# ScalarE seeds an accumulating PSUM bank with the first of seven products, and VectorE's first add falls away

## The chip, the cores and the metric

The kernel runs on one core of one Trainium2 chip. The metric is the device time of one execution in microseconds (us), lower is better. The kernel is written by hand in a low-level language: every instruction is issued to one engine (TensorE, ScalarE, VectorE, GpSimd, or SyncE for transfers), each engine executes its own instructions in order, and engines wait for each other through semaphores.

## The reference

Linformer attention followed by a gated feed-forward layer, in float32:

```
k_proj = einsum('ks,bhsd->bhkd', E, k)         # 8 batches, 8 heads, 1024 tokens, 64 per head
v_proj = einsum('ks,bhsd->bhkd', F, v)
attn   = softmax(q @ k_proj^T / 8)
x      = (attn @ v_proj), heads joined         # 8192 tokens x 512
gate   = 1 / (1 + exp(-(x @ w_gate)))          # 512 x 1536
val    = x @ w_val                             # 512 x 1536
out    = (gate * val) @ w_out                  # 1536 x 512
```

## The kernel before, in words

The kernel multiplies in bf16 and accumulates in fp32 in PSUM. PSUM has eight banks, each holding a 128 x 512 fp32 tile. Four of them, pF0 to pF3, serve the feed-forward layer; pA0 to pA3 serve attention and the output product.

The 8192 tokens are cut into 16 blocks of 512. Block 0 goes through the feed-forward layer plainly (`mstep`: 12 steps, each with a G product and a V product of four matmuls, then `gate`). For blocks 1 to 15 the value product x @ w_val is done by a Strassen-like scheme: a block and the weights are cut into 2 x 2 parts, and seven products of sums replace eight. The sums of x lie in `xS`, those of the weights in `vT` and in part of `wV`. One *group* K (3 to 47, 45 groups, three to a block) makes four of the twelve 128-row strips of the hidden layer, and `v_pieces(K)` writes its seven products as five pieces. Two banks, called a and c in the code, are held through the group:

- p1: product A11·B11 into bank a (four matmuls of 256 columns). `v_snap(0, a)`: ScalarE copies a into the SBUF tile `vsnap0`. Bank a keeps its contents, and later products accumulate onto it.
- p26: product A12·B21 into bank c; `v_add(0, c)`: VectorE adds bank c to `vsnap0`. Then S2·T2 onto bank a and `v_snap(1, a)`. Then `hidden(K, 0, 0)`: VectorE multiplies the finished quarter by its gate and writes a quarter of `hT`.
- p57: S1·T1 into bank c, from the start; S3·T3 onto a; `v_snap(2, a)`; `v_add(2, c)`.
- p4: A22·T4 onto a; `hidden(K, 0, 1)` straight from bank a; `hidden(K, 1, 1)` from `vsnap2`.
- p3: S4·B22 onto c; `v_add(1, c)`; `hidden(K, 1, 0)` from `vsnap1`.

Between these pieces stand the gate products `g_step(K, n)`, n = 0 to 3: four matmuls of 512 columns into a bank of their own, and a tanh on ScalarE into a `sig` tile. The order on TensorE around a group is p3 of the group before, p1, g1, p26, g2, p57, g3, p4, g0 of the next group, p3. That order is written out by hand in `quad_pieces`, and `on(u, j, ...)` hangs other work behind chosen pieces: attention's scores, their exponentials and products (`scores3`, `mixed3`, `outputs3`), VectorE's sums for later blocks (`x_sums`, `h_sums`), and the output product, which is also done with seven products (`first_products`, `last_products`, 24 matmuls each before the next piece).

The banks pF0 to pF3 are handed out by a first-in-first-out list `FF`: `take()` takes the head, `two()` takes two, and a step appends its bank when it has emitted the instruction that reads it last. The list fixes, while the program is built, which earlier reader a bank's next writer waits for. `Plan.add` derives those waits from the keys of each operation. In its argument list, `x` marks a bank that an operation uses alone, `r` a key that it reads and `w` a key that it writes. All matmuls are recorded under line 264 and all ScalarE operations under line 268 (helpers `mm` and `act`), `v_add` under L1476, `hidden` under L1457, `gate` of block 0 under L1133.

Of the kernel before, what the change touches and what calls it, by code (L numbers as in the profile page):

```python
# [6 lines left out]
AF = mybir.ActivationFunctionType  # L7
# [20 lines left out]
class Plan:  # L28
# [9 lines left out]
    def add(self, eng, fn, r=(), w=(), x=(), dma=None):  # L38
        op = Op()
        op.eng, op.fn, op.dma, op.need = eng, fn, dma, False  # L40
        op.sem, op.val = None, 0
        deps = {}

        def dep(o, raw):
            if o is op:
                return
            if o.eng == eng and o.dma is None:
                if eng == "PE" or (eng != "POOL" and not raw):
                    return
            deps[id(o)] = o  # L50

        for k in r:
            for o in self.writers.get(k, ()):
                dep(o, True)
        for k in tuple(w) + tuple(x):
            for o in self.writers.get(k, ()):
                dep(o, False)
            for o in self.readers.get(k, ()):
                dep(o, False)
        for k in r:  # L60
            self.readers.setdefault(k, []).append(op)
        for k in tuple(w) + tuple(x):
            self.writers[k] = [op]
            self.readers[k] = []
        op.deps = list(deps.values())
        for o in op.deps:
            o.need = True
        if dma is not None:
            self.dma_count[dma] = self.dma_count.get(dma, 0) + 16
            op.sem, op.val = dma, self.dma_count[dma]  # L70
        self.ops.append(op)
        return op
# [46 lines left out]
def bass_linformer_attn__then__ffn_glu_sigmoid_kernel(  # L119
# [18 lines left out]
    with contextlib.ExitStack() as es:  # L138

        def sbuf(name, shape, dtype):  # L140
            return es.enter_context(nc.sbuf_tensor(name, shape, dtype))
# [7 lines left out]
        def within(shape, dtype):  # L149
# [64 lines left out]
        vsnap = [sbuf(f"vsnap{i}", [P, 512], FP32) for i in range(3)]  # L214
        xS = [sbuf(f"xS{i}", [P, 4, 2, 256], BF16) for i in range(2)]

        bank = [
            es.enter_context(nc.psum_tensor(n, [P, 512], FP32))
            for n in ("pF0", "pF1", "pF2", "pF3", "pA0", "pA1", "pA2", "pA3")
        ]  # L220
# [3 lines left out]
        add = plan.add  # L224
# [29 lines left out]
        FF, AA = Free(), Free()  # L254

        def mm(b, o, lhsT, rhs, r, start=True, stop=True, tp=None, tr=False, read=False):
            kw = {"skip_group_check": True} if read else {}
            if tp is not None:
                kw["tile_position"] = tp
            if tr:  # L260
                kw["is_transpose"] = True
            else:
                kw["start"], kw["stop"] = start, stop
            return add("PE", lambda e: e.matmul(o, lhsT, rhs, **kw), r=r, x=[("bank", b)])  # L264

        def act(o, i, r, w, b=None, func=AF.Copy, scale=1.0):
            x = [] if b is None else [("bank", b)]
            return add("ACT", lambda e: e.activation(o, i, func, scale=scale), r=r, w=w, x=x)  # L268

        def dve(fn, r, w, b=None):  # L270
            x = [] if b is None else [("bank", b)]
            return add("DVE", fn, r=r, w=w, x=x)
# [807 lines left out]
        def chunk(m):  # L1080
            return max(x for x in range(len(WCH) - 1) if WCH[x] <= m * P)
# [319 lines left out]
        def x_part(blk, n):  # L1401
            s, hf = blk // 2 % 2, blk % 2
            if n[0] == "S":
                return xS[blk % 2][:, int(n[1]) - 1, :, :], [("xS", blk % 2, int(n[1]))]
            tok, i0 = int(n[1]) - 1, 2 * (n[2] == "2")
            return (
                xT[s][:, i0 : i0 + 2, hf, 256 * tok : 256 * tok + 256],
                [("xT", s, i0 + i, hf, tok) for i in range(2)],
            )
# [11 lines left out]
        def v_product(blk, q, bk, A, B, start=False, stop=False):  # L1421
            x, kx = x_part(blk, A)
            for j in range(2):
                for i in range(2):
                    m = 2 * q + j
                    if B in ("T2", "T3", "T4"):
                        w, kw = vT[:, int(B[1]) - 2, i, m * P : (m + 1) * P], ("vT", int(B[1]), int(m > 1))
                    else:
                        if B == "T1":
                            ii, mm_, kw = i, m + H6, ("vT", 1, int(m > 1))  # L1430
                        else:
                            ii, mm_ = i + 2 * (B[1] == "2"), m + H6 * (B[2] == "2")
                            kw = ("wV", chunk(mm_), ii // 2)
                        w = wV[:, ii, mm_ * P : (mm_ + 1) * P]
                    mm(
                        bk,
                        bank[bk][:, 256 * j : 256 * j + 256],
                        w,
                        x[:, i, :],
                        kx + [kw],  # L1440
                        start=start and i == 0 and j == 0,
                        stop=stop and i == 1 and j == 1,
                        read=True,
                    )

        def pair(k, half_):
            return sigs[(2 * k + half_) % 3], ("sig", (2 * k + half_) % 3)

        def hidden(K, half_, tok, x, r, b=None):

            blk, q = K // 3, K % 3
            m = 2 * q + H6 * half_
            sg, k = pair(K, half_)
            cc = slice(256 * tok, 256 * tok + 256)
            o = hT[blk % 2][:, m : m + 2, cc]
            dve(
                lambda e: e.scalar_tensor_tensor(  # L1457
                    o,
                    sg[:, :, cc],
                    1.0,  # L1460
                    x.rearrange("p (j c) -> p j c", j=2),
                    ALU.add,
                    ALU.mult,
                ),
                [k + (j,) for j in range(2)] + r,
                [("hT", blk % 2, m + j, tok) for j in range(2)],
                b=b,
            )

        def v_snap(n, bk):  # L1470
            act(vsnap[n][:, :], bank[bk][:, :], [], [("vsnap", n)], b=bk)

        def v_add(n, bk):
            o = vsnap[n][:, :]
            dve(
                lambda e: e.tensor_tensor(o, bank[bk][:, :], o, ALU.add),  # L1476
                [("vsnap", n)],
                [("vsnap", n)],
                b=bk,
            )  # L1480

        held_v = {}
# [19 lines left out]
        def v_pieces(K):  # L1502
            blk, q = K // 3, K % 3

            def p1():
                held_v["a"] = a = FF.take()
                v_product(blk, q, a, "A11", "B11", start=True)
                v_snap(0, a)

            def p26():  # L1510
                a = held_v["a"]
                held_v["c"] = c = FF.take()
                v_product(blk, q, c, "A12", "B21", start=True, stop=True)
                v_add(0, c)
                v_product(blk, q, a, "S2", "T2")
                v_snap(1, a)
                hidden(K, 0, 0, vsnap[0][:, :], [("vsnap", 0)])

            def p57():
                a, c = held_v["a"], held_v["c"]  # L1520
                v_product(blk, q, c, "S1", "T1", start=True)
                v_product(blk, q, a, "S3", "T3")
                v_snap(2, a)
                v_add(2, c)

            def p4():
                a = held_v["a"]
                v_product(blk, q, a, "A22", "T4", stop=True)
                hidden(K, 0, 1, bank[a][:, :], [], b=a)
                FF.append(a)  # L1530
                hidden(K, 1, 1, vsnap[2][:, :], [("vsnap", 2)])

            def p3():
                c = held_v["c"]
                v_product(blk, q, c, "S4", "B22", stop=True)
                v_add(1, c)
                FF.append(c)
                hidden(K, 1, 0, vsnap[1][:, :], [("vsnap", 1)])

            return p1, p26, p57, p4, p3  # L1540


# [165 lines left out]
        for b in range(1, B):  # L1708
            todo, at = [], {}
            for u in range(6):  # L1710
                K = 6 * b + u
# [116 lines left out]
```

The softmax here doesn't subtract the row's maximum and nothing guards it: scores larger than these inputs give would overflow.

## Time and profile before

| | |
|---|---|
| median of 9 runs | 531.78 us (530.67 to 533.45) |
| the profiled execution, its own time | 531.3 us |
| its span | 529.5 us |
| TensorE matmul (PE) busy | 519.1 us, 98% of the span, 4173 instructions |
| VectorE (DVE) busy | 416.3 us, 79%, 681 instructions |
| ScalarE (ACT) busy | 307.1 us, 58%, 551 instructions |
| granted TensorE clock | full speed in all 40 slices |
| `v_snap` copies (ACT, `vsnap<-pF`) | 135, 80.7 us, mean 598 ns |
| `v_add` (DVE, L1476) | 135, 93.0 us, mean 689 ns |
| `hidden` from an SBUF tile (DVE, L1457, `hT<-sig,vsnap`) | 135, 93.5 us, mean 693 ns |
| `hidden` from a bank (DVE, L1457, `hT<-sig,pF`) | 45, 30.8 us, mean 685 ns |

In the profile PE is the matmul stream and PEld the weight loads, which run ahead of it; a wait of TensorE stands at the weight load. A matmul's record lasts longer than its turn, because matmuls are pipelined: starts follow each other every 109 ns for 256 columns and every 216 ns for 512 columns, so that a v product takes 0.44 us and a gate product 0.86 us of TensorE's time. In the timeline a line may stand for several instructions of one kind (xN), with the start of the first and the time that they cover; an idle time before it is given in brackets with what ended it.

### The profile page before, as it was taken

The numbers are of one execution on the slowest core, as the hardware profiler recorded it, in microseconds if no ns is written. First come the engines' busy times: TensorE is split into PE (matmuls) and PEld (weight loads), VectorE is DVE, ScalarE is ACT, GpSimd is POOL, SyncE is SP. The second block draws the span as 40 slices with busy tenths as digits, with TensorE's granted clock in tenths as the row PEclk, the third lists the DMA queues.
The fourth block names the chain that finished last, engine by engine and source line by source line (L and its number), as shares of the span: only waits on it lengthen the run. The fifth ranks groups of instructions, "written<-read, shape, count | busy, mean of one in ns | idle before, by whom it ended". The sixth has DMA issues, their size and how long they took to land.

```text
span 529.5 us, 10478 instructions
## 1 busy us (share of the span) xinstructions
PE 519.1 (98%) x4173; PEld 351.2 (66%) x4173; DVE 416.3 (79%) x681; ACT 307.1 (58%) x551; POOL 133.4 (25%) x148
## 2 busy tenths in 40 slices
PE   5999999999999999999999999999999999999997
PEld 4545646656857667585766767576685867677676
DVE  4649786788987788877988779877888788997855
ACT  2665753688385564946468474764838564554641
POOL 9310200106700085001920048100650009200000
PEclk9999999999999999999999999999999999999999
DMA  9999999994293255911589213962620020202022
GB/s 170 199 199 202 154 213 190 185 174 87 34 230 62 82 91 82 232 51 41 90 155 163 80 36 60 211 106 80 83 91 1 0 82 4 80 1 79 1 81 80
DMA packets 77153, 56.18 MB, mean 106 GB/s; under 512 B 34800, under 2 KB 69296, under 8 KB 77104
## 3 DMA queue, kind: packets, MB, share of 16 engines
q0 software_dynamic: 33984, 29.89, 36.5%
q1 hardware_dynamic: 43120, 25.63, 19.6%
q8 instruction: 32, 0.52, 0.4%
q14 instruction: 17, 0.14, 0.1%
HBM read 60.29 MB, written 16.78 MB: 146 GB/s over the span
## 4 chain that ended last, share of the span: by engine, by line
PE 97%; DVE 1%; DMA 1%; ACT 1%; issue 0%; SPq 0%
PE pF L264 64%; PE pA L264 33%; DMA EF<-in_F_dram 1%; DVE vsnap L1476 0%; ACT vsnap L268 0%; DVE rden L639 0%; ACT vpD L268 0%; DVE hT L1457 0%; ACT qT L268 0%; SPq L350 0%; DVE vpD L541 0%; DVE ost L1338 0%; ACT wT L268 0%
## 5 line engine op out<-in xcount | busy, mean ns | idle before, releaser
L264 PE MATMUL pF<-xT,wG 128*128 128x512 bf16 x768 | 197.5, 379 | 0.3
L926 POOL PARTITION_BROADCAST KVs<-eT x96 | 96.8, 1034 | 243.5 <-PE pF L264 190.7
L268 ACT ACTIVATE sig<-pF 128x512 f32<-128x512 f32 x192 | 115.4, 601 | 49.2 <-PE pF L264 47.2
L1476 DVE TENSOR_TENSOR vsnap<-pF,vsnap 128x512 f32<-128x512 f32 x135 | 93.0, 689 | 39.8 <-PE pF L264 29.5
L264 PEld LDWEIGHTS pF<-xT,wG 128*128 128x128 bf16 x768 | 74.2, 98 | 54.4 <-issue 1.7
L268 ACT ACTIVATE vsnap<-pF 128x512 f32<-128x512 f32 x135 | 80.7, 598 | 46.9 <-PE pF L264 42.4
L1457 DVE SCALAR_TENSOR_TENSOR hT<-sig,vsnap 128x512 bf16<-128x512 f32 x135 | 93.5, 693 | 6.2
L264 PE MATMUL pF<-xT,wV 128*128 128x256 bf16 (+1 forms) x408 | 66.9, 286 | 0.0
L264 PE MATMUL pA<-wO,hT 128*128 128x256 bf16 x534 | 63.4, 273 | 0.0
L264 PEld LDWEIGHTS pA<-wO,hT 128*128 128x128 bf16 x534 | 52.1, 98 | 6.6 <-DVE ost L1267 0.3
L264 PE MATMUL pF<-xS,wV 128*128 128x256 bf16 x360 | 54.1, 273 | 0.3
L264 PEld LDWEIGHTS pF<-xT,wV 128*128 128x128 bf16 x408 | 38.2, 98 | 23.9 <-issue 5.7
L264 PE MATMUL pF<-xS,vT 128*128 128x256 bf16 x360 | 54.0, 273 | 0.0
L264 PEld LDWEIGHTS pF<-xS,wV 128*128 128x128 bf16 x360 | 34.3, 98 | 25.6 <-DVE vsnap L1476 5.0
L958 DVE TENSOR_TENSOR xT<-xu,KVs 128x512 bf16<-128x512 f32 x48 | 47.3, 1022 | 1.2 <-POOL KVs L926 0.7
L268 ACT ACTIVATE EF<-pA 128x512 f32<-128x512 f32 x30 | 17.9, 597 | 46.9 <-PE pA L264 46.9
L264 PE MATMUL pA<-wT,hT 128*128 128x256 bf16 x360 | 44.2, 273 | 0.0
L264 PE MATMUL pA<-wT,hS 128*128 128x256 bf16 x360 | 41.7, 273 | 0.0
L264 PEld LDWEIGHTS pA<-wT,hT 128*128 128x128 bf16 x360 | 35.1, 98 | 7.3 <-ACT snap L268 0.3
L264 PEld LDWEIGHTS pA<-wT,hS 128*128 128x128 bf16 x360 | 35.1, 98 | 4.3 <-issue 0.2
L264 PEld LDWEIGHTS pF<-xS,vT 128*128 128x128 bf16 x360 | 35.2, 98 | 4.1
L1267 DVE SCALAR_TENSOR_TENSOR ost<-pA,EF 128x512 f32<-128x512 f32 x29 | 20.0, 688 | 19.8 <-PE pA L264 19.8
(113 smaller groups left out, 488.6 us busy)
## 6 DMA issues: line engine op xcount, KB each, us to landing
out_dram<-ost SPq DMA_DIRECT2D x60, 256.0 KB, 2.4
Qb<-in_q_dram POOLq DMA_DIRECT2D x7, 1024.0 KB, 20.2
KVs<-in_k_dram POOLq DMA_DIRECT2D x7, 1024.0 KB, 12.1
KVs<-in_v_dram POOLq DMA_DIRECT2D x7, 1024.0 KB, 16.0
wO<-in_moe_w_out_dram POOLq DMA_DIRECT2D x1, 1536.0 KB, 12.7
wG<-in_moe_w_gate_dram POOLq DMA_DIRECT2D x5, 256.0 KB, 17.6
wV<-in_moe_w_val_dram POOLq DMA_DIRECT2D x5, 256.0 KB, 18.2
KVs<-in_k_dram POOLq DMA_DIRECT2D x2, 512.0 KB, 7.8
```

The source lines that it names most:

```text
L264: return add("PE", lambda e: e.matmul(o, lhsT, rhs, **kw), r=r, x=[("bank", b)])
L268: return add("ACT", lambda e: e.activation(o, i, func, scale=scale), r=r, w=w, x=x)
L926: lambda e, n=n, i=2 * rnd + c, j=j, parts=parts: e.partition_broadcast(rb[0:parts, n, :], rrow[32 * j : 32 * j + 1, i, :], channels=parts),
L958: lambda e: e.tensor_tensor(xT[s][:, r, :, 256 * g : 256 * g + 256], xu[:, n, :].rearrange("p (f c) -> p f c", f=2), y.rearrange("p (f c) ...
L1267: lambda e: e.scalar_tensor_tensor(o, bank[bk][:, :].rearrange("p (j c) -> p j c", j=2), 0.5, snap[n].rearrange("p (j c) -> p j c", j=2), ...
L1457: lambda e: e.scalar_tensor_tensor(o, sg[:, :, cc], 1.0, x.rearrange("p (j c) -> p j c", j=2), ALU.add, ALU.mult,),
L1476: lambda e: e.tensor_tensor(o, bank[bk][:, :], o, ALU.add),
```

## The change

In p1, bank c is taken together with bank a, and ScalarE copies the finished first product into bank c instead of `vsnap0` (`v_seed`). The matmuls of A12·B21 then accumulate onto bank c without a start flag. VectorE's `v_add(0, c)` is gone, and `hidden(K, 0, 0)` reads its values from bank c instead of `vsnap0`. The other products, copies and adds stay, and so does the written order of the pieces. Since c leaves the list `FF` one piece earlier, the later takers of banks get other banks than before.

```diff
+        def v_seed(a, c):
+            add(
+                "ACT",
+                lambda e: e.activation(bank[c][:, :], bank[a][:, :], AF.Copy, scale=1.0),
+                r=[("bank", c)],
+                x=[("bank", a), ("bank", c)],
+            )
...
             def p1():
-                held_v["a"] = a = FF.take()
+                held_v["a"], held_v["c"] = a, c = FF.two()
                 v_product(blk, q, a, "A11", "B11", start=True)
-                v_snap(0, a)
+                v_seed(a, c)

             def p26():
-                a = held_v["a"]
-                held_v["c"] = c = FF.take()
-                v_product(blk, q, c, "A12", "B21", start=True, stop=True)
-                v_add(0, c)
+                a, c = held_v["a"], held_v["c"]
+                v_product(blk, q, c, "A12", "B21", stop=True)
                 v_product(blk, q, a, "S2", "T2")
                 v_snap(1, a)
-                hidden(K, 0, 0, vsnap[0][:, :], [("vsnap", 0)])
+                hidden(K, 0, 0, bank[c][:, :], [], b=c)
```

## The prediction

> **What bounds the kernel now.** I read the page first, its busy times and the chain that ended last.
>
> ```profile
> PE 519.1 (98%) x4173; PEld 351.2 (66%) x4173; DVE 416.3 (79%) x681; ACT 307.1 (58%) x551; POOL 133.4 (25%) x148
> ...
> PE 97%; DVE 1%; DMA 1%; ACT 1%; issue 0%; SPq 0%
> ```
>
> TensorE's stream sets the end, and VectorE's work lies beside it. So the 45 adds that fall away (45 x 0.689 = 31.0 us of VectorE's 416.3) are worth only what TensorE waits for VectorE. The change is priced by the waits of TensorE that go and those that come. For that I took the instructions in order of time, group by group. First group 33, which stands for the plainest kind:
>
> ```profile
> 369.92 0.61 PE L264 MATMUL pF<-xT,wV 128*128 128x256 bf16 x4
> ...
> 370.37 1.03 PE L264 MATMUL pF<-xT,wG 128*128 128x512 bf16 x4
> ...
> 370.63 0.60 ACT L268 ACTIVATE vsnap<-pF 128x512 f32<-128x512 f32 x1 [1.56 <-PE pF L264]
> ...
> 371.23 0.60 PE L264 MATMUL pF<-xT,wV 128*128 128x256 bf16 x4
> ```
>
> The first product ends at 370.53, ScalarE's copy starts 0.10 later and ends at 371.23, and the second product starts at 371.23. Today it needs nothing from that copy. Now group 34, from the end of its g0 on:
>
> ```profile
> 376.31 0.58 ACT L268 ACTIVATE sig<-pF 128x512 f32<-128x512 f32 x1
> ...
> 376.88 1.03 PE L264 MATMUL pF<-xT,wG 128*128 128x512 bf16 x4
> 377.14 0.60 ACT L268 ACTIVATE vsnap<-pF 128x512 f32<-128x512 f32 x1 [0.25 <-PE pF L264]
> ...
> 377.76 0.59 ACT L268 ACTIVATE vpD<-pA 64x512 bf16<-64x512 f32 x1
> ...
> 378.38 0.60 ACT L268 ACTIVATE sig<-pF 128x512 f32<-128x512 f32 x1
> 378.45 0.69 DVE L1476 TENSOR_TENSOR vsnap<-pF,vsnap 128x512 f32<-128x512 f32 x1 [0.39 <-PE pF L264]
> ...
> 379.48 0.60 PE L264 MATMUL pF<-xS,wV 128*128 128x256 bf16 x4
> ...
> 380.61 0.59 ACT L268 ACTIVATE vsnap<-pF 128x512 f32<-128x512 f32 x1
> ...
> 381.25 0.33 PEld L264 LDWEIGHTS pF<-xT,vT 128*128 128x128 bf16 x4 [0.37 <-ACT vsnap L268]
> 381.26 0.61 PE L264 MATMUL pF<-xT,vT 128*128 128x256 bf16 x4
> ...
> 382.73 0.33 PEld L264 LDWEIGHTS pF<-xS,wV 128*128 128x128 bf16 x4 [0.49 <-DVE vsnap L1476]
> ```
>
> The lines near 381 give the price of a release: the copy ends at 381.20, the held weight load starts 0.05 later, its matmul 0.01 after that, and the gap to the next matmul is 0.01 too long. I count 0.065 us from a release to a matmul. Third, the start of group 3:
>
> ```profile
> 46.27 1.03 PE L264 MATMUL pF<-xT,wG 128*128 128x512 bf16 x4
> ...
> 46.51 0.68 DVE L1133 SCALAR_TENSOR_TENSOR hT<-sig,pF 128x512 bf16<-128x512 f32 x1
> ...
> 47.24 0.33 PEld L264 LDWEIGHTS pF<-xT,wV 128*128 128x128 bf16 x4 [0.44 <-DVE hT L1133]
> ```
>
> **The change part by part.** *The copy into bank c* keeps its place, its two waits (TensorE and VectorE, hence the 0.10 before it) and its count. No row has ScalarE writing PSUM. From below: `vpD<-pA` takes 271 ns at 128 columns and 594 at 512, 0.84 ns a column, so 431 ns is the streaming and 166 the fixed part; the copy can't be shorter than 431. From above: the fixed part twice, 763. I take the nearest row, the same copy to SBUF, 597 ns: all ScalarE rows of 512 columns lie at 592 to 601, whether they write bf16 or fp32.
>
> *The new wait of the second product for the copy.* Today the first reader of a copy's release is S2·T2, 0.44 us later; now the second product has only g1 (0.86) as cover. The line-up by group, copy end plus 0.065 against the second product's start:
> - 13 groups (4, 5, 7, 8, 9, 15, 21, 27, 33, 40, 43, 45, 46) are like 33: 371.23 + 0.065 against 371.23, or 0.06 each: 0.77.
> - 13, 19, 25, 31: two exponentials hold the copy up. In 31 it ends at 346.04, the product started at 345.98: 0.12 each, 0.48. Group 37 has 0.07; 39 has 0.24 (copy until 432.22, product at 432.04).
> - 14 groups (6, 11, 14, 17 and so on to 47) have 24 matmuls of the output product between g1 and p26, 2.6 us: nothing.
> - 12, 18, 24, 30, 36 are below, as are 3, 10, 16, 22, 28, 34 and 42.
>
> *The banks' order.* With c taken early, g1 gets the bank of the group's own g0 (or one from the attention work), not that of the group before.
> - In 12, 18, 24, 30, 36, g1 waits today for `v_add(1)` of the group before, 0.20 us. That bank becomes c, and g1 gets one that the first exponential has released. Then the copy is last: in 30 it ends at 338.45, so 338.52 against 338.60 today. From unrounded starts, -0.07 four times and -0.12 in 36: -0.42.
> - Group 3 is the first with the list, and g1 now gets the bank that the last `gate` of block 0 still reads. That is the third block above: this VectorE operation holds the second product until 47.24 today. Then g1 starts there instead of at 46.27, and the second product a gate product (0.86) after it: +0.86, once. S1·T1 follows in step, since VectorE is done before.
>
> *The wait of S1·T1 for `hidden(K, 0, 0)`*, which reads bank c; today it waits for `v_add(0)`. `hidden` also needs g1's tanh. Where the tanh is early this costs nothing: in 33 it ends 1.95 after the last matmul of p1 starts, `hidden` 0.03 + 0.69 later, with 0.065 that is 2.74, and S1·T1, itself 0.06 later, starts at 2.77. Price without this cover: a microsecond for a microsecond. It fails in 10, 16, 22, 28 and 34, where `vpD` stands before the tanh: in 34 that ends at 378.98, `hidden` at 379.70, S1·T1 starts at 379.77 instead of 379.48, +0.29. (Also g1 there waits 0.07 for g0's tanh, inside that 0.29.) But p4 and p3 of these groups wait today, 0.05 and 0.17 beyond their turn, for ScalarE's third copy and for `v_add(2)`, which stands behind two multiplications; those start 0.24 sooner, as `hidden` does. So 0.29 - 0.05 - 0.17 leaves 0.07, x5 = 0.32 from unrounded rows.
>
> *The add that falls away.* VectorE gets to what is queued behind it (h and x sums, multiplications, `v_add(2)`) up to 0.69 sooner, never later, since `hidden` now starts before its old start in every group. `hidden` from a bank is 685 ns against 693: nothing. TensorE's other waits on VectorE: in 42, S1·T1 waits 0.19 behind a full VectorE queue; with two adds fewer the queue is empty in time, 0.19 goes and the 0.06 of the copy comes: -0.15 with rounding. In 14 and 41 the waits (0.09, 0.19, 0.13) hang on TensorE and on GpSimd's broadcasts, and stay.
>
> Sum: 0.77 + 0.48 + 0.07 + 0.24 - 0.42 + 0.86 + 0.32 - 0.15 = +2.2 us. The profiled execution (531.3, its span 529.5 and 1.8 around it) becomes 533.5. It lies 0.5 below the median, so I add the 2.2 to the median: 534.0.
>
> The copy's length weighs most, because 29 groups hang on its end: 0.029 us of total for each ns. At 431 the thirteen pay nothing, 39 keeps 0.08, the five with exponentials gain 0.19 each and the five with `vpD` 0.10 each, 42 gains 0.2, group 3 still pays 0.86: -0.7, or 531.1. At 763 the sum is about +7, or 539.
>
> A rule of the Trainium skill speaks here: "Perfetto Trace Analysis", section "Optimizing Scalar/DVE Operations", gives ScalarE about 93 ns of access overhead on SBUF and about 51 on PSUM. No row of this trace shows a write to PSUM; by the page the copy would be an estimated 42 ns shorter, 555, and the total +1.0 instead of +2.2.
>
> Against the change itself speaks "PSUM — Partial Sum Buffer", section "The four PSUM rules": engine writes don't touch the bits that decide whether a matmul adds or overwrites, so a seed counts only where an earlier matmul left the bit set. Either way the time is the same.
>
> **The rivals.** The bound for a difference is 0.2%, 1.06 us, about what a measurement of this kernel can tell from no change.
> - *No change: the copy into PSUM is short.* From 558 ns down the sum falls under 1.06; at 431 it is -0.7. Time 531.1 to 532.8. For: the copy moves no byte to SBUF. Against: 592 to 601 whatever is written. Chance 0.30.
> - *Slower by far more: reading and writing PSUM in one instruction costs the fixed part twice.* 536 to 539. Against: nothing in the trace shows it. Chance 0.08, within the slower case.
> - *Faster: VectorE's 31 us come back on top of a short copy.* TensorE's waits on VectorE that I hold fixed (groups 14 and 41 above, and 0.28 each in 5 and 47, where no gate product covers `v_add(2)`) sum to 0.97; with the -0.7 that gives 530.1. It decides only if both hold. Against: in 5 and 47 VectorE idles before that add, waiting for ScalarE. Chance 0.06.
> - *The first product isn't kept*, because the matmuls overwrite the seed: the same 534.0, by the same instructions.
>
> **How the numbers follow.** The likeliest case, slower by over 0.2%, has 0.64, the short copy 0.30, faster 0.06. The range runs from 531.8 (a copy of some 520 ns) to 535.9 (some 660 ns, 0.029 x 65 above the point) and leaves out the far ends.
>
> **What would show it.** The group of `vsnap` copies falls to 90; a row of 45 copies from pF to pF appears, and its mean settles the largest term: 597 or well below. PEld waits on that copy in some 25 groups, ending with a second product 0.06 to 0.24 late. S1·T1 waits for L1457 in 10, 16, 22, 28, 34. In group 3, g1 waits near 1 us for L1133. L1476 falls to 90 and VectorE to some 385 us, with the span longer. I am wrong if the span is shorter by a microsecond, if group 3's g1 starts at its old place, or if the copy's row is far from 597.

## The result and the profile after

| | before | after |
|---|---|---|
| median | 531.96 us (30 runs, 530.67 to 534.75) | 533.81 us (10 runs, 533.03 to 534.17; an eleventh on record took 534.70) |
| span of the profiled execution | 529.5 us | 531.9 us |

The ratio is 1.0031, with a 95% interval of 1.002 to 1.0043. The changed kernel is slower by some 1.7 us (1.1 to 2.3). The forecast was 534.0.

The page of the changed kernel, its span, busy times and the row of the new copy:

```profile
span 531.9 us, 10389 instructions
...
PE 520.5 (98%) x4173; PEld 346.6 (65%) x4173; DVE 386.9 (73%) x636; ACT 307.9 (58%) x551; POOL 128.6 (24%) x148
```

```profile
L1476 ACT ACTIVATE pF<-pF 128x512 f32<-128x512 f32 x45 | 26.6, 591 | 11.0 <-PE pF L264 11.0
```

VectorE lost 29.4 us of work, and the span grew all the same. The copy from bank to bank takes 591 ns, 6 less than to SBUF. The waits of the weight loads (us in total, times, longest) name the new link:

```profile
PEld pF L264 <- ACT pF L1476: 11.2, 30, 0.4
PEld pF L264 <- DVE hT L1457: 8.6, 26, 0.5
```

In thirty groups a weight load waits for the copy. In six of them (4, 10, 16, 22, 28, 34) g1 is itself late by about as much, so that the second product stands in its turn behind it; in the other 24 it starts late. These totals count the idle time of the weight loads, most of which matmuls hide. What TensorE loses is read from the starts of the matmuls. First group 33, in order of time:

```profile
372.81 0.58 ACT L1476 ACTIVATE pF<-pF 128x512 f32<-128x512 f32 x1 [1.55 <-PE pF L264]
...
373.44 0.33 PEld L264 LDWEIGHTS pF<-xT,wV 128*128 128x128 bf16 x4 [0.36 <-ACT pF L1476]
373.45 0.61 PE L264 MATMUL pF<-xT,wV 128*128 128x256 bf16 x4
```

The gate product between starts at 372.55 and takes 0.86, so this product's turn was at 373.41. It starts 0.03 to 0.04 late, held by the copy that ends at 373.39. Group 34, where `vpD` stands before the tanh:

```profile
380.59 0.60 ACT L268 ACTIVATE sig<-pF 128x512 f32<-128x512 f32 x1
...
381.22 0.69 DVE L1457 SCALAR_TENSOR_TENSOR hT<-sig,pF 128x512 bf16<-128x512 f32 x1 [0.94 <-ACT sig L268]
...
381.96 0.33 PEld L264 LDWEIGHTS pF<-xS,wV 128*128 128x128 bf16 x4 [0.52 <-DVE hT L1457]
```

VectorE sits idle for 0.94 until the tanh ends at 381.19, then `hidden` runs until 381.91, and S1·T1 is released by it. And group 3:

```profile
47.34 0.68 DVE L1133 SCALAR_TENSOR_TENSOR hT<-sig,pF 128x512 bf16<-128x512 f32 x1
...
48.08 1.04 PE L264 MATMUL pF<-xT,wG 128*128 128x512 bf16 x4 [0.82 <-DVE hT L1133]
```

The gate product stands still for 0.82 us of idle matmul time until block 0's last `gate` has left its bank.

TensorE issues the same 4173 matmuls in the same order in both kernels, so their starts can be laid side by side. By group, from the start of its g0 to that of the next group's, after minus before, in us:

| groups | difference | |
|---|---|---|
| 3 | +0.86 | bank of block 0's last gate |
| 5 | -0.40 | +0.05 for the copy; the rest is explained below |
| 7, 8, 9, 15, 21, 27, 33, 40, 43, 45, 46 | +0.04 to +0.06 each | copy |
| 4 | +0.05 | bank order: g1 waits for g0's tanh |
| 13, 19, 25, 31; 37; 39 | +0.12 each; +0.07; +0.24 | copy behind other ScalarE work; in 39 g1 alone is 0.13 late by the bank order |
| 12, 18, 24, 36; 30 | -0.07 to -0.12; +0.20 | bank order and copy |
| 10, 16, 22, 28, 34, to the end of their p3 | +0.04 to +0.05 each | `hidden` behind the tanh |
| 14, 41, 42 | -0.10, -0.12, -0.16 | S1·T1 waits less (0.09, 0.13, 0.19); in 42 0.03 for the copy |
| the others | 0.00 | |

From group 3's g0 to the end this sums to +1.52. A further 0.83 of the 2.35 us by which the last matmul is later comes from before that point, where the change has no instruction.

### The profile page after: what moved, and what is told of

Same layout as the page of the kernel before. It is cut to its first block, busy times and chain, and to the rows that moved or that the text cites. A ratio compares the mean times of both kernels' runs of the same rounds, so it can differ in the third digit from the quotient of the medians.

```text
span 531.9 us, 10389 instructions
## 1 busy us (share of the span) xinstructions
PE 520.5 (98%) x4173; PEld 346.6 (65%) x4173; DVE 386.9 (73%) x636; ACT 307.9 (58%) x551; POOL 128.6 (24%) x148
## 4 chain that ended last, share of the span: by engine, by line
PE 94%; DMA 2%; DVE 2%; POOL 1%; ACT 0%; issue 0%; DVEq 0%; POOLq 0%
PE pF L264 62%; PE pA L264 32%; DMA KVs<-in_v_dram 2%; DVE xT L691 0%; DVE hT L1133 0%; POOL KVs L282 0%; POOL Qb L282 0%; DVE vsnap L1484 0%; ACT vsnap L268 0%; DVE rden L639 0%; ACT vpD L268 0%; ACT eT L268 0%; DVE vT L1399 0%; DVE vpD L541 0%; DVE ost L1338 0%
## 5 line engine op out<-in xcount | busy, mean ns | idle before, releaser
L926 POOL PARTITION_BROADCAST KVs<-eT x96 | 92.0, 984 | 244.0 <-PE pF L264 190.3
L264 PEld LDWEIGHTS pF<-xT,wG 128*128 128x128 bf16 x768 | 72.8, 98 | 56.8 <-issue 1.7
L1484 DVE TENSOR_TENSOR vsnap<-pF,vsnap 128x512 f32<-128x512 f32 x90 | 62.0, 689 | 48.9 <-PE pF L264 32.1
L1457 DVE SCALAR_TENSOR_TENSOR hT<-sig,pF 128x512 bf16<-128x512 f32 x90 | 61.7, 685 | 25.8 <-PE pF L264 19.3
L268 ACT ACTIVATE vsnap<-pF 128x512 f32<-128x512 f32 x90 | 53.7, 597 | 36.2 <-PE pF L264 34.1
L1457 DVE SCALAR_TENSOR_TENSOR hT<-sig,vsnap 128x512 bf16<-128x512 f32 x90 | 62.7, 696 | 1.5
L264 PEld LDWEIGHTS pF<-xT,wV 128*128 128x128 bf16 x408 | 35.9, 98 | 27.8 <-ACT pF L1476 11.2
```

Of the source, the lines that this page charges most:

```text
L926: lambda e, n=n, i=2 * rnd + c, j=j, parts=parts: e.partition_broadcast(rb[0:parts, n, :], rrow[32 * j : 32 * j + 1, i, :], channels=parts),
L1457: lambda e: e.scalar_tensor_tensor(o, sg[:, :, cc], 1.0, x.rearrange("p (j c) -> p j c", j=2), ALU.add, ALU.mult,),
```

## The experiments

Times are compared with the kernel before as ratios. Since one ratio is known to about 0.1%, each experiment is read mainly from the matmul starts of its trace, group by group, as above.

**The bank order alone.** The kernel before with only this edit:

```diff
-                held_v["a"] = a = FF.take()
+                held_v["a"], held_v["c"] = a, c = FF.two()
...
-                held_v["c"] = c = FF.take()
```

> The kernel before with one part of the change alone: bank c is taken in p1 together with a, but the copy to vsnap0, v_add(0) and the SBUF form of hidden stay. Theory (each new or vanished wait of TensorE is paid where it stands): group 3's g1 starts 0.98 us late and its second product 0.86; at the output product of block 0, where TensorE waits for the load of wO, some 0.48 of that is absorbed; g1 in groups 12, 18, 24, 30, 36 starts about 0.19 sooner each (-0.95); g1 in 39 starts 0.12 later; the second product waits for no copy. Sum about -0.4 us against the kernel before. Rival (the bank order is what costs, the copy's waits are hidden): +1.8 us or nearly all of the change's loss, with the second products late by 0.03 to 0.10 here too.

Ratio 0.9998 (0.9989 to 1.0008). In the trace group 3 has +0.86, groups 12, 18, 24, 30 have -0.19 and 36 -0.22, 39 has +0.13, the five `vpD` groups +0.07 and 4 has +0.05 (g1 waiting for g0's tanh), 41 has -0.30. No second product is late, and at the output product of block 0 TensorE waits 0.48 less than in the kernel before. The starts sum to -0.3. So the early bank costs nothing in this trace, and group 3's 0.86 is shown to be the bank's, not the copy's. Without the 0.48 and without group 41, which varies between traces (below), the sum would be about +0.5.

**Group 3 with the late bank.** The changed kernel with this ahead of p1's and p26's new text (for K = 3 the old text, then return):

```diff
+                if K == 3:
+                    held_v["a"] = a = FF.take()
+                    v_product(blk, q, a, "A11", "B11", start=True)
+                    v_snap(0, a)
+                    return
```

> The changed kernel with group 3 alone done as before (c taken late, copy to vsnap0, v_add). Theory: group 3's second product starts 0.86 us sooner, but TensorE then waits again for the load of wO at the output product of block 0, so that 0.4 to 0.5 of it is lost there and the whole gains about 0.4 us against the changed kernel. Rival (the 0.48 that the output product of block 0 gained came from VectorE's lighter queue): the whole 0.86 us is gained.

Ratio 1.0018 (1.0007 to 1.0029), against the changed kernel's 1.0031. Against that kernel's trace group 3 gains 0.86 and every other group is where it was, but for 0.28 later in 12 and 0.28 sooner in 30. The wait for wO did not come back in this trace: TensorE came to block 0's output product at 72.1 us, 0.8 later than in the changed kernel's trace, because its first 45 us had run 1.7 us slower. The trace thus follows the rival's number, but not its cause: the bank order alone gained the 0.48 with all of VectorE's adds in place. What the place is worth on average is open (below).

**VectorE's load put back.** The changed kernel with an add that nobody waits for, behind `hidden(K, 0, 0)`:

```diff
                 hidden(K, 0, 0, bank[c][:, :], [], b=c)
+                sg, k = pair(K, 0)
+                dve(
+                    lambda e: e.tensor_tensor(vsnap[0][:, :], sg[:, 0, :], sg[:, 1, :], ALU.add),
+                    [k + (j,) for j in range(2)],
+                    [("vsnap", 0)],
+                )
```

> The changed kernel with one extra VectorE add of two sig halves into vsnap0 behind hidden(K, 0, 0) in each group, which nobody waits for: VectorE's load is that of the kernel before again. Theory (TensorE waits for VectorE in few places only): the S1.T1 waits of groups 14, 41 and 42 come back, 0.4 us together, and p3 of groups 10, 16, 22, 28, 34 waits 0.2 to 0.4 each for v_add(2) behind the multiplications: +1.4 to +2.4 us against the changed kernel, all of it in these eight groups. Rival (what TensorE saves comes from the order of the waits, not from VectorE's lighter queue): within 0.3 us of the changed kernel.

Ratio 1.0105 (1.009 to 1.012), some 4 us above the changed kernel. Against its trace the five `vpD` groups lose 0.70 each at their p3 and nothing else loses anything; groups 14 and 42 stay where the change had put them. Group 34 in order of time:

```profile
384.73 1.08 DVE L1526 TENSOR_TENSOR vsnap<-sig 128x512 f32<-128x512 f32 x1
...
385.73 2.22 DVE L958 TENSOR_TENSOR xT<-xu,KVs 128x512 bf16<-128x512 f32 x2
...
387.87 0.68 DVE L1484 TENSOR_TENSOR vsnap<-pF,vsnap 128x512 f32<-128x512 f32 x1
...
388.60 0.33 PEld L264 LDWEIGHTS pF<-xS,wV 128*128 128x128 bf16 x4 [1.02 <-DVE vsnap L1484]
```

The extra add (1.08 us here) pushes the two multiplications, they push `v_add(2)`, and p3 waits for that. So VectorE's queue sets TensorE's pace in five places of 45. The expectation had the place right and the size too small by half. It was wrong on 14, 41 and 42: their waits on S1·T1 did not come back (41 even gained 0.22). The add put back is not quite the one taken away. It stands behind `hidden`, so it can't delay the S1·T1 of its own group, and in these five groups it takes 1.08 where `v_add(0)` took 0.69; so 0.70 is more than the old add cost there.

**`hidden` taken off the bank.** In the changed kernel VectorE copies bank c to `vsnap0` in the place of the old add:

```diff
+                dve(lambda e: e.tensor_scalar(vsnap[0][:, :], bank[c][:, :], 1.0, None, op0=ALU.mult),
+                    [], [("vsnap", 0)], b=c)
...
-                hidden(K, 0, 0, bank[c][:, :], [], b=c)
+                hidden(K, 0, 0, vsnap[0][:, :], [("vsnap", 0)])
```

> The changed kernel, but VectorE copies the finished bank c into vsnap0 (in v_add(0)'s place, 0.69 us) and hidden(K, 0, 0) reads vsnap0, so that S1.T1 no longer waits for hidden and g1's tanh. Theory: S1.T1 in groups 10, 16, 22, 28, 34 starts 0.19 sooner, but p4 and p3 there wait again (0.04 and 0.16), so these groups end within 0.05 of where they were; the waits of 14, 41 and 42 come back, +0.4 us; the second products stay as late as in the changed kernel. Sum +0.2 to +0.5 us against the changed kernel. Rival (hidden's wait on the tanh is the main cost): -0.9 us.

Ratio 1.0044 (1.003 to 1.0058): not told apart from the changed kernel by time. In its trace S1·T1 of the five `vpD` groups starts 0.19 sooner, p4 waits 0.04 and p3 0.10 more, and the groups end 0.05 sooner. Group 42 gets 0.13 of its wait back, so this wait does hang on what VectorE does ahead of `hidden`; 14 and 41 get none, and 41 gains 0.22 elsewhere. As expected, the wait on the tanh is paid back two products later. The sum was not as expected: -0.3 by the starts, -0.1 without group 41, for +0.2 to +0.5.

**The copy issued twice.**

```diff
                 v_seed(a, c)
+                v_seed(a, c)
```

> The changed kernel with the copy into bank c issued twice in a row; the second repeats the first. Back-to-back ScalarE copies start some 0.48 us apart, so the second product's release comes 0.48 later. Theory (in 29 groups the second product hangs on the copy's end with no slack; in the 14 groups with 24 matmuls between, and in group 42 partly, it is covered): +0.4 to +0.5 us in each of the 29 to 31 groups and nothing in the 14, +12 to +16 us against the changed kernel. Rival (the lateness of 0.03 to 0.1 is a fixed cost of a cross-engine wait and not the copy's end): +1 to +3 us, from ScalarE's longer queue.

Ratio 1.035 (1.0314 to 1.0387), 551.54 us (2 runs). Group 33 in its trace:

```profile
384.50 1.20 ACT L1476 ACTIVATE pF<-pF 128x512 f32<-128x512 f32 x2 [1.56 <-PE pF L264]
...
385.74 0.33 PEld L264 LDWEIGHTS pF<-xT,wV 128*128 128x128 bf16 x4 [0.97 <-ACT pF L1476]
385.75 0.61 PE L264 MATMUL pF<-xT,wV 128*128 128x256 bf16 x4 [0.48 <-ACT pF L1476]
```

Thirty groups lose, 28 of them 0.61 to 0.62 each. Group 28 loses 0.91 and group 30 only 0.34, because a late start of some 0.28 (last section) falls in 28 here and in 30 in the changed kernel's trace. Group 3 and the covered groups lose nothing (41 gains 0.18). That is 18.2 us against the changed kernel's trace, above the 12 to 16 expected. The count is the theory's 29 with group 42. The step per group is 0.61 and not 0.48, because the second copy waits for the first to end (the code lists bank c as read); they don't overlap.

**Cover for the copy.** The changed kernel with p1 issued ahead of the p3 of the group before, in the eleven groups that have no attention work between:

```diff
+        AHEAD = {4, 10, 16, 22, 28, 34, 40, 42, 43, 45, 46}
...
+            first = [before, p1] if K not in AHEAD else [lambda: (p1(), before()), lambda: None]
```

(`before` is the p3 of the group before, which `quad_pieces` now takes; `held_v` is kept per group.)

> The changed kernel with one edit: in groups 4, 10, 16, 22, 28, 34, 40, 42, 43, 45, 46 p1 is issued ahead of the p3 of the group before. Theory (the loss is the missing cover of 0.06 us and of the tanh behind vpD): the second products of these groups start in turn (-0.03 each), S1.T1 of the five vpD groups waits no more for hidden (-0.19 each), and what is left there is the gain at p4 and p3: -1.1 to -1.3 us against the changed kernel. Rival (p3 and the banks that it frees, now later, become the wait): the same time or slower.

Ratio 1.0004 (0.999 to 1.0017), against 1.0031. In all eleven groups the second product now starts in its turn. By the matmul starts the `vpD` groups gain 0.15 each and 42, 43, 45, 46 0.04 each; 4 gains nothing, since its g1 is late, and 40 loses 0.05, since the p3 issued there waits. With 0.22 in group 41, which varies between traces, the sum is -1.04; without it -0.8, less than the 1.1 to 1.3 expected.

**A version that beats both.** The same order of p1 and p3; the copy into the bank only where it is covered; elsewhere the old copy and add, with the bank taken early except in 3 and 39:

```diff
+        COVERED = {6, 11, 14, 17, 20, 23, 26, 29, 32, 35, 38, 41, 44, 47}
+        SEED, LATE = AHEAD | COVERED, {3, 39}
...
+                if K in SEED:
+                    v_seed(a, held_v["c"])
+                else:
+                    v_snap(0, a)
...
+                v_product(blk, q, c, "A12", "B21", start=K not in SEED, stop=True)
+                if K not in SEED:
+                    v_add(0, c)
```

> A version built from what the waits showed. In groups 4, 10, 16, 22, 28, 34, 40, 42, 43, 45, 46 (no attention work between p3 and p1) p1 is issued ahead of the p3 of the group before, so that p3 and g1 together cover the copy, which goes into bank c as in the change. In the 14 groups with 24 matmuls of the output product after g1 the change stays. In the others the copy goes to vsnap0 and v_add(0) stays, with bank c taken early (late in 3 and 39). Theory: no second product waits for a copy; g1 in 12, 18, 24, 30, 36 starts 0.19 sooner (-0.95); groups 10, 16, 22, 28, 34 lose 0.06 at g1 and gain 0.2 at p4 and p3 (-0.7); the S1.T1 waits of 14, 41, 42 go (-0.3). About -2.0 us against the kernel before, 0.4% faster. Rival (the seed has a cost of its own beyond these waits): not faster than the kernel before.

Ratio 0.9968 (0.9942 to 0.9994), median 530.71 us. Group 34 again, in order of time:

```profile
376.85 0.60 PE L264 MATMUL pF<-xT,wV 128*128 128x256 bf16 x4
...
377.28 0.60 PE L264 MATMUL pF<-xS,wV 128*128 128x256 bf16 x4
...
377.62 0.59 ACT L1476 ACTIVATE pF<-pF 128x512 f32<-128x512 f32 x1
...
377.78 1.04 PE L264 MATMUL pF<-xT,wG 128*128 128x512 bf16 x4
...
378.66 0.60 PE L264 MATMUL pF<-xT,wV 128*128 128x256 bf16 x4
```

The first product now stands before p3, and the copy ends at 378.21, well ahead of the second product's turn at 378.66. The starts show what was expected: -0.19 to -0.22 in 12, 18, 24, 30, 36; +0.07 at g1 and -0.18 at p3 in the `vpD` groups; -0.10, -0.34 and -0.20 in 14, 41 and 42; nothing in the groups with the old copy. Against that stands +0.47 in group 5 of this trace, the wait for wO. The starts sum to -1.59, or -2.06 without that wait, for about -2.0 expected; of 41's 0.34, 0.19 belongs to a wait that varies between traces. In this version 25 of the 45 VectorE adds are gone.

## Why the prediction was right

*The copy's length.* The nearest row, the same copy to SBUF, gave 597 ns; it was 591. (The two `vpD` rows are 270 and 593 ns, not 271 and 594; the slope is the same.) The Trainium skill's "Perfetto Trace Analysis", section "Optimizing Scalar/DVE Operations", gives ScalarE's overhead by memory space, without saying whether the source or the destination counts. Taken for the destination, its figures make the copy an estimated 42 ns shorter, 555. The measured row decides: 6 of those 42 ns are there.

*The second product's wait.* Right in the 14 groups without it, and in 28 of the 29 with it. Group 4 was put down to the copy, and there the bank order had already made g1 as late. The plain groups lost 0.04 to 0.06 where 0.06 was forecast, since their copies took 0.58 to 0.60. The copy issued twice shows that all these groups hang on its end: none has more than 0.04 of slack.

*The bank order.* Group 3 (+0.86) and g1 of 12, 18, 24, 36 are right to 0.02; the bank order alone shows both. In 39 the copy's 0.24 covers a g1 that is 0.13 late. Group 30 missed, +0.20 for -0.07: its exponentials started 0.28 late in this trace (last section), and no term of the sum had that.

*`hidden` behind the tanh.* S1·T1 was held as forecast in the five groups named; they ended 0.04 to 0.05 later, for 0.07 forecast.

*The add that falls away.* Group 42 is right (-0.16 for -0.15). The step had two misses on S1·T1, small and both gains: it kept group 14's wait, which went (0.09), and 41's, of which 0.13 went. Neither is shown to come from VectorE's lighter load. With the load put back both stay gone, and 41's shrank by 0.10 in the bank order alone, which has every add. In 14, `v_add(0)` started 0.25 to 0.27 later in the traces of the kernel before and of the bank order alone than in the groups like it; no kernel without that add shows this. Why is open.

The prediction also did not see that the output product of block 0 waits in the kernel before for the load of wO:

```profile
69.98 0.13 PEld L264 LDWEIGHTS pF<-wO,hT 128*128 128x128 bf16 x2 [0.68 <-DVE vsnap L1476]
```

The profile names VectorE here. But these matmuls wait in the code for the load of wO and for an earlier VectorE operation, and TensorE's own record shows a wait for the load's semaphore until 69.96, just before this weight load. In the trace after, TensorE gets there at 71.3 and the wait of 0.48 is gone. That is not all the change's doing. The load had landed at 69.72, so even without group 3's 0.86 TensorE would have come after it, because the first 45 us ran 0.83 longer there. In the bank order alone it was group 3's delay that hid the wait: TensorE came at 70.1, and 0.86 sooner would have been ahead of the load, which landed at 69.54.

*The sum.* Forecast +2.2 on the median; measured +1.7 (1.1 to 2.3) by the ratio and +1.52 by the matmul starts from group 3 on. Without the 0.48 at wO the starts would give +2.0, and without the late start in group 30 as well +1.7. These two misses partly cancel, which is luck. Most of the 0.5 that is left lies in the plain groups (0.2), in 14 and 41 (0.2) and in the tanh's term (0.1). So the mechanism was right in its main terms, and the sum came out somewhat high.

*The rivals.* The short copy (no change) fell with the 591 ns. A copy that pays the fixed part twice fell with it. VectorE's 31 us coming back did not happen: with the load put back, five places react, and the change had already taken their waits at p3 (0.16 each). The last rival, a seed that the matmuls overwrite, had the same time as the forecast, so no time here bears on it.

What stays open: how often the wait for wO is paid. It was 0.48 in the trace of the kernel before, 0.95 in the last version's and nil in the other seven, whose first 45 us ran between 0.35 less and 2.5 us longer. Moving that load was not tried.

## What to carry to other kernels

On an engine that is 98% busy, price a change by the stalls that it moves, one by one in program order, and not by the work it takes off another engine. When a result is handed on earlier in the chain (copy before product instead of add after it), look at what stands between producer and consumer: here the first product ended 0.16 us after the start of a gate product of 0.86, and 0.16 + 0.10 + 0.59 + 0.065 is 0.05 more than that covers. A 0.44 us product moved in between covered the same copy in all eleven groups where it was tried. Holding a buffer longer changes who gets which buffer next; follow the list by hand, above all at its first use.

## What the runs showed of the hardware

Two dependent ScalarE copies of 128 x 512 took 1.20 us together, while independent ones in these traces mostly follow each other every 0.48 to 0.50 us.

A VectorE add of two SBUF tiles that takes 0.68 us in 39 groups took 1.07 to 1.08 us in the six where it ran beside GpSimd's broadcasts.

In eight of the nine traces one operation that waits for TensorE was seen to start 0.25 to 0.29 us later than its like in other groups. It was `v_add(0)` of group 14 in the kernel before and in the bank order alone. It was ScalarE's first exponential of group 30 in the changed kernel and in three variants, that of group 12 in the one with group 3's late bank, and the copy of group 28 where it is issued twice. So it may depend on the program and not on the run; why was not found.

The first 45 us of the execution, before any changed instruction, varied from trace to trace by nearly 3 us, more than the whole effect; per-group differences of the matmul starts resolved 0.04 us.
